# RetNet attention and a SwiGLU block on one core: the RMS norm's sum over partitions taken by VectorE block turns and one 16-column product

## The chip, the cores and the metric

The kernel runs on one NeuronCore of one Trainium2 chip. The metric is the device time of one launch in microseconds (us). Before the change three runs gave 1104.73 us as their median (1101.4 to 1110.42).

The engines are named as the profile names them: PE is TensorE (PEld its loading of weights), DVE is VectorE, ACT is ScalarE, POOL is GpSimd, SP is SyncE, which here only issues transfers. Each engine works through its own queue in the order in which the program issued to it.

## What is computed

```python
# q, k, v: (8, 8, 576, 64); tokens 4608, d_model 512, d_ff 1536, all float32
scores = scale * q @ k.T;  ret = scores * Dmat           # per head, decay matrix
attn   = ret @ v                                          # then (B,H,S,D) -> x (4608, 512)
rms = sqrt(mean(x * x, axis=-1) + 1e-6)
xn  = x / rms * rms_g
g = xn @ w_gate;  val = xn @ w_val
out = (g * sigmoid(g) * val) @ w_out
```

The part that changes is the middle one: for each token, the sum of the squares of its 512 features, the reciprocal root of that sum, and the multiplication of x by it and by `rms_g`.

## The kernel before, in words

**Layout.** The 4608 tokens are cut into nine units of 512 (`u` = 0 to 8). A unit's x lies in on-chip memory as `[128, 4, 512]`: the 512 features are four chunks of 128 partitions, the tokens run along the columns. A sum over a token's features is therefore a sum over four chunks, which adding four tiles does, and over 128 partitions, which no column-wise operation does.

**Attention.** 32 jobs (8 batches, 4 pairs of heads). A job's `slot` (L431) issues the values of the job before, its own scores and states to PE, then `weigh` (L320) and `sums` (L334) to DVE, and `carried` (L391), whose last step copies into x. For the first eight jobs (units 0 and 1) q and k are turned by PE (`turn`, L222).

**The feed-forward part.** Units 0 and 1 multiply with plain weights (`up_plain`, L694) while the same weights are rounded and prepared on the fly (`rounding`, L1191, whose steps `exponent` on ACT, `mantissa` and `join` on DVE handle 36 half blocks one after the other; after every fourth `join` of an up block, POOL adds the block's sums, L1130). Units 2 to 8 use a product scheme with seven instead of eight sub-products: `up` (L635) has six rounds of seven products, `across` (L781) has seven products of the output matrix. In `across`, POOL makes the sums of the left operands (`inner_sums`, L759) and DVE adds the results.

**The norm before, units 2 to 8.** `square` (L456, ACT) and `gather` (L464, DVE) give one `[128, 512]` tile with a row of partial sums in each partition. `root_1` (L499) multiplies it on PE by a matrix of ones, `[128,128] x [128,512]`, so that every partition holds every token's sum; then ACT and DVE compute a reciprocal root on all 512 columns by an integer guess and steps of an iteration (ACT L506, L509, L516; DVE L510, L513, L517); `root_2` (L522) has the last two DVE operations (L526, L529). `scale_x` (L537) multiplies the four chunks of x by the result (L548), which lies in on-chip SBUF, and `sums_of_x` (L553) makes the sums for the next unit's `up`.

**The norm before, units 0 and 1.** `norm_1` (L476): eight PE products of one column each (L481) turn the sums so that tokens lie on partitions; ACT adds epsilon (L486), POOL takes the power -0.5 (L487), `diagonals` (L490, ACT, L495) spreads the 4 columns over four diagonal matrices, and `scale_x` multiplies ones by them on PE (L546) so that PSUM holds the rows, which L548 reads.

**What sets the order.** There is no scheduler: queues run in the order of issue. For units 0, 1 and the first half of unit 2's preparation the order is the string `PLAN` (L1158), read word by word: `T` turn, `S` slot, `C` close, `Q` square, `G` gather, `N` norm_1, `D` diagonals, `X` scale_x, `U` up_plain (unit, block, quarter), `w` one step of the rounding, `a` one ACT step of it, `A` one product of `across`, `R` root_1, `Y` root_2, `M` sums_of_x, `k` the constant `rms_k`. For the units after that the loop at L1282 sets it: in the last round of `up` the four squares and gathers ride on the first four products, `root_1(u + 1)` on the fifth (i == NHP), and in `across` `root_2(u + 1)` comes at i == 2, the four `scale_x` at i = 3 to 6, `sums_of_x` at i == 8.

**PSUM.** Eight banks of 512 columns are handed out in turn (`bank`, L89); a bank that was freed earliest is given next.

Of the kernel before, what the change touches and what calls it, by code (L numbers as in the profile page):

```python
# [10 lines left out]
F32 = mybir.dt.float32  # L11
U32 = mybir.dt.uint32
AF = mybir.ActivationFunctionType
# [31 lines left out]
def kernel(  # L45
# [56 lines left out]

    ones = const.tile([P, P], F32, name="ones")
    ident = const.tile([P, P], F32, name="ident")
    mean_w = cell("mean_w", 1.0 / DM)
    mhalf = cell("mhalf", -0.5)
    eps = cell("eps", EPS)
    most = cell("most", 1151.0 + 7.5 / 16)
    top = cell("top", 255.0 * 2.0**23)
    guess = cell("guess", 0x5F1FFFF9 + 2.0**22 * np.log2(DM))  # L110
# [364 lines left out]

    def norm_1(u):  # L476

        ms = bank(f"ms_{u}")
        for s in range(NS):
            for i, sq in enumerate(t_of[u]):  # L480
                nc.tensor.matmul(  # L481
                    ms[:, s : s + 1], lhsT=sq[:, s * P : s * P + P], rhs=mean_w,
                    start=(i == 0), stop=(i == 1),
                )
        r = tmp.tile([P, NS], F32, tag="r", name=f"r_{u}", bufs=1)
        nc.scalar.activation(out=r, in_=ms[:, :NS], func=AF.Relu, bias=eps)  # L486
        nc.gpsimd.tensor_tensor(out=r, in0=r, in1=mhalf.to_broadcast([P, NS]), op=ALU.pow)  # L487
        t_of[u] = r

    def diagonals(u):  # L490

        r = t_of[u]
        t_of[u] = row(f"diag_{u}")
        for s in range(NS):
            nc.scalar.activation(  # L495
                out=t_of[u][:, s * P : s * P + P], in_=ident, func=AF.Copy, scale=r[:, s : s + 1]
            )

    def root_1(u):  # L499


        y = t_of[u]
        s = bank(f"ms_{u}")
        nc.tensor.matmul(s, lhsT=ones, rhs=y, start=True, stop=True)
        e = row(f"e_{u}")
        nc.scalar.activation(  # L506
            out=y.bitcast(U32), in_=s.bitcast(U32), func=AF.Relu, bias=guess, scale=-0.5
        )
        nc.scalar.activation(out=e, in_=y, func=AF.Square)  # L509
        nc.vector.scalar_tensor_tensor(  # L510
            out=e, in0=e, scalar=-1.0 / DM, in1=s, op0=ALU.mult, op1=ALU.mult
        )
        nc.vector.scalar_tensor_tensor(  # L513
            out=y, in0=e, scalar=K0, in1=y, op0=ALU.add, op1=ALU.mult
        )
        nc.scalar.activation(out=e, in_=y, func=AF.Square)  # L516
        nc.vector.scalar_tensor_tensor(  # L517
            out=e, in0=e, scalar=K1 * K1 / DM, in1=s, op0=ALU.mult, op1=ALU.mult
        )
        t_of[u] = y, e  # L520

    def root_2(u):  # L522


        y, e = t_of[u]
        nc.vector.scalar_tensor_tensor(  # L526
            out=e, in0=e, scalar=-10.0 / 3.0, in1=e, op0=ALU.add, op1=ALU.mult
        )
        nc.vector.scalar_tensor_tensor(  # L529
            out=y, in0=e, scalar=5.0, in1=y, op0=ALU.add, op1=ALU.mult  # L530
        )
        t_of[u] = y

    def norm_2(u):
        scale_x(u, range(NHP))
# [1 line left out]
    def scale_x(u, chunks):  # L537


        x = x_of[u]  # L540
        g = rms_k
        rb = t_of[u]
        if u < 2:
            g = rms_g
            rb = bank(f"rb_{u}")
            nc.tensor.matmul(rb, lhsT=ones, rhs=t_of[u], start=True, stop=True)  # L546
        for c in chunks:
            nc.vector.scalar_tensor_tensor(  # L548
                out=x[:, c], in0=x[:, c], scalar=g[:, c : c + 1], in1=rb,
                op0=ALU.mult, op1=ALU.mult,  # L550
            )

# [598 lines left out]
    def store_blocks(n):  # L1151
# [4 lines left out]

    IN_PSUM = range(4, 36)
    PLAN = """  # L1158
        T0 V0 a1 S0 a1 T1 a1 a1 V1 S1 T2 V2 F8 S2 V3 T3 w1 a1 w1 Q0 a1 a1 G0 Q1 a1 S3 T4 G1 V4
        a1 a1 w1 Q2 a1 S4 a1 V5 w1 T5 G2 V6 Q3 a1 a1 G3 a1 S5 w1 T6 V7 w1 Q4 a1 S6 N0 a1 w1 a1  # L1160
        D0 a1 a1 G4 a1 T7 a1 w1 a1 w1 a1 a1 a1 Q5 X0 G5 S7 w1 U000 w1 a1 a1 a1 Q6 a1 C7 G6 a1 Q7
        G7 U001 N1 w1 w1 w1 D1 U002 w1 a1 X1 a1 w1 a1 w1 w1 w1 w1 a1 a1 a1 w1 a1 U003 a1 w1 w1
# [11 lines left out]
        G9 b1 i4 Q10 k0 Q11 a1 b2 A0 i5 A0 a1 a1 G10 A0 j6 A0 A0 A0 a1 P12 A0 j7 b3 A0 j8 c2 A1  # L1174
        c0 F13 A1 v1 A1 c3 A1 j9 o0 G11 A1 A1 j10 A1 A1 j11 A1 i12 A1 R2 A1 Y2 A1 X2 M2 p1 a1 a1
        i13 A1 A1 A1 A1
    """
    TAILS = ((0, range(2)), (0, range(2, H)), (1, range(2)), (1, range(2, H)))
# [51 lines left out]
    def start():  # L1230

        tables = list(zip((causal, gv, gc, gq, gp), (_causal_table(), *_decay_tables(H, D))))

        def table(i, queue):
            t, values_ = tables[i]
            src = nc.inline_tensor(values_, name=t.tensor.name + "_table")
            queue.dma_start(out=t, in_=src.ap())

        make_identity(nc, ident)
        nc.scalar.activation(out=tick, in_=mhalf[:1], func=AF.Silu)  # L1240
        nc.vector.memset(ones, 1.0)
# [15 lines left out]
        tasks = {  # L1257
            "S": lambda j: slot(j, rest=j not in (0, FIRST)), "C": close, "T": turn, "V": scale_v,
            "P": prepare, "F": fetch, "Q": lambda j: squares.append(squared(*divmod(j, NHP))),
            "G": lambda j: gather(*squares.pop(0)), "N": norm_1, "D": diagonals, "X": norm_2,  # L1260
            "w": weights, "a": act, "d": lambda f: differences(f // 3, 2 * (f % 3)),
            "i": lambda n: inner_sums(*divmod(n, 7)),
            "j": lambda n: inner_sums(*divmod(n, 7), eng=nc.vector),
            "c": lambda b: combine(b, nc.gpsimd), "v": combine,
            "b": lambda n: (second_operand, last_operand)[n % 2](n // 2),
            "z": lambda n: store_blocks(len(halves) + 9),
            "r": refill, "W": weights_to, "A": lambda u: next(outs[u], None), "R": root_1,
            "Y": root_2, "M": sums_of_x, "o": store, "p": lambda _: later.pop()(),
            "k": lambda _: nc.vector.tensor_scalar(
                out=rms_k, in0=rms_g, scalar1=3.0 / 8.0 * K1, scalar2=None, op0=ALU.mult  # L1270
            ), "U": lambda n: up_plain(n // 100, n // 10 % 10, n % 10),
        }
# [7 lines left out]
    with tc.manual_schedule():  # L1280
        start()
        for u in range(2, NU):  # L1282
            j0 = NHP * (u + 1)
            more = u + 1 < B
            for n in range(2 * NG):
                for i, _ in enumerate(up(u, n)):
# [57 lines left out]
```

## Time and profile before

| | |
|---|---|
| Runs | 1104.73 us median of 3 (1101.4 to 1110.42) |
| Profiled execution | span 1104.5 us from the first to the last instruction; its own time isn't listed apart from the three runs, the median of which is 0.2 us above the span |
| Mean granted clock of TensorE | 0.995 |
| DMA | 243.60 MB, mean 221 GB/s |
| Products of the sevenfold scheme (L644) | 672 + 672 + 672 + 336 records of 256 columns, about 380 ns each as shown |
| Plain products (L704) | 384 records of 512 columns, 595 ns each as shown |

A float32 product stands in the trace as two PE records, and records overlap, so that their durations add up to more than the time they take; what a stretch of products takes is read from the distance of the starts. The row of a group gives its count, busy time and mean, then how long its engine idled just before it and what ended that.

### The profile page before, as it was taken

To read this page: it belongs to the slowest core of one execution; us is meant where nothing else is said; L and a number is where in the kernel's file an instruction comes from. 1 tells how busy PE (TensorE), PEld (TensorE's weight loads), DVE (VectorE), ACT (ScalarE), POOL (GpSimd) and SP (SyncE) were. 2 spreads that over 40 slices of the span, in tenths; PEclk is the share of its full clock that TensorE was granted. 3 is DMA by queue.
4 is the path that set the end of the run, shared out by engine and by line. 5 is a ranking of instruction groups with operands and counts; after the bars stand their busy time and mean duration, and the time that the engine had idled before them with its cause. 6 is when DMAs were issued, how large, how long until landed. Compare 5 with 4: busy or idle time off the path is not lost.

```text
span 1104.5 us, 24454 instructions
## 1 busy us (share of the span) xinstructions
PE 1091.5 (99%) x10102; PEld 915.1 (83%) x10102; DVE 751.7 (68%) x1219; ACT 339.7 (31%) x757; POOL 458.0 (41%) x421
## 2 busy tenths in 40 slices
PE   8899999999999999999999999999999999999998
PEld 7654444479988899889988998889888998898898
DVE  3778568877866794678657775668565935594457
ACT  5855564331124412342034303330233111211110
POOL 0026325538430196027802581239321942393236
PEclk9899999999999999999999999999999999999999
DMA  8847777696978866787678865887475755585461
GB/s 211 197 139 259 280 244 217 208 343 185 289 277 227 216 251 226 185 238 235 253 215 199 285 259 149 245 246 284 143 203 198 273 193 176 183 293 158 152 247 43
DMA packets 253871, 243.60 MB, mean 221 GB/s; under 512 B 193216, under 2 KB 213824, under 8 KB 247616
## 3 DMA queue, kind: packets, MB, share of 16 engines
q1 hardware_dynamic: 252320, 241.64, 69.1%
q8 instruction: 79, 1.29, 0.5%
q10 hardware_dynamic: 1440, 0.40, 0.2%
q14 instruction: 32, 0.26, 0.1%
HBM read 211.92 MB, written 30.08 MB: 219 GB/s over the span
## 4 chain that ended last, share of the span: by engine, by line
PE 96%; DVE 1%; issue 1%; ACT 0%; POOL 0%; POOLq 0%; DVEq 0%; ACTq 0%
PE up L704 15%; PE x L644 14%; PE w L644 13%; PE z L644 13%; PE y L644 7%; PE xo L814 6%; PE xp L814 4%; PE zo L814 4%; PE zp L814 3%; PE wo L814 2%; PE yo L814 2%; PE av L379 2%; PE wp L814 2%; PE av L399 2%; PE s L292 2%; PE yp L814 2%
## 5 line engine op out<-in xcount | busy, mean ns | idle before, releaser
L704 PE MATMUL up<-x,ring 128*128 128x512 f32 x384 | 167.1, 595 | 0.0
L644 PE MATMUL x<-x,ring 128*128 128x256 f32 x672 | 161.1, 383 | 0.0
L644 PE MATMUL w<-sums,ring 128*128 128x256 f32 x672 | 158.9, 379 | 0.0
L644 PE MATMUL z<-x,ring 128*128 128x256 f32 x672 | 158.8, 379 | 0.0
L766 POOL TENSOR_TENSOR vi<-h 128x384 f32<-128x384 f32 x32 | 39.5, 1234 | 275.2 <-DVE h L663 266.3
L704 PEld LDWEIGHTS up<-x,ring 128*128 128x128 f32 x384 | 72.3, 190 | 89.3 <-issue 84.8
L644 PEld LDWEIGHTS z<-x,ring 128*128 128x128 f32 x672 | 127.8, 190 | 19.8 <-issue 2.9
L644 PEld LDWEIGHTS w<-sums,ring 128*128 128x128 f32 x672 | 127.7, 190 | 17.2
L644 PEld LDWEIGHTS x<-x,ring 128*128 128x128 f32 x672 | 125.5, 190 | 17.4 <-ACT m L670 0.2
L771 POOL TENSOR_TENSOR vi<-h 128x384 f32<-128x384 f32 (+2 forms) x46 | 46.4, 1009 | 149.5 <-DVE h L663 149.5
L1010 POOL TENSOR_TENSOR vi<-vi 128x512 f32<-128x512 f32 (+1 forms) x77 | 78.1, 1027 | 37.9 <-DVE vi L841 21.5
L644 PE MATMUL y<-sums,ring 128*128 128x256 f32 x336 | 79.4, 379 | 0.0
L670 ACT COPY m<-x 128x512 f32<-128x512 f32 x42 | 24.6, 586 | 173.4 <-PE x L644 173.4
L651 DVE TENSOR_TENSOR h<-u,w 128x512 f32<-128x512 f32 x42 | 28.9, 688 | 67.8 <-PE w L644 67.8
L651 DVE TENSOR_TENSOR u<-m,y 128x512 f32<-128x512 f32 x42 | 28.8, 687 | 63.4 <-PE y L644 62.7
L644 PEld LDWEIGHTS y<-sums,ring 128*128 128x128 f32 x336 | 63.9, 190 | 8.6
L665 ACT ACTIVATE h<-h 128x512 f32<-128x512 f32 x63 | 39.7, 630 | 84.1 <-DVE h L651 84.1
L1130 POOL TENSOR_TENSOR vi<-vi 128x512 f32<-128x512 f32 (+1 forms) x24 | 40.7, 1696 | 30.8 <-DVE vi L1119 17.3
L651 DVE TENSOR_TENSOR u<-u,z 128x512 f32<-128x512 f32 x42 | 28.9, 688 | 33.7 <-PE z L644 33.6
L1130 POOL TENSOR_TENSOR ring<-ring 128x512 f32<-128x512 f32 x24 | 30.4, 1272 | 49.3 <-DMA w_up_blocks<-ring 44.1
L771 POOL TENSOR_TENSOR vi<-vi,h 128x384 f32<-128x384 f32 (+2 forms) x46 | 47.6, 1034 | 3.6
L771 POOL TENSOR_TENSOR vi<-h,vi 128x384 f32<-128x384 f32 (+2 forms) x46 | 46.9, 1019 | 3.6
(314 smaller groups left out, 2086.5 us busy)
## 6 DMA issues: line engine op xcount, KB each, us to landing
ring<-w_out_blocks SPq DMA_DIRECT2D x59, 1344.0 KB, 6.4
ring<-w_up_blocks SPq DMA_DIRECT2D x42, 1792.0 KB, 7.7
w_out_blocks<-vi SPq DMA_DIRECT2D x21, 448.0 KB, 5.9
out_dram<-vi SPq DMA_DIRECT2D x64, 128.0 KB, 3.0
qraw<-in_q_dram SPq DMA_DIRECT2D x96, 72.0 KB, 5.1
kraw<-in_k_dram SPq DMA_DIRECT2D x96, 72.0 KB, 2.5
k<-in_k_dram SPq DMA_DIRECT2D x48, 128.0 KB, 2.9
v<-in_v_dram SPq DMA_DIRECT2D x48, 128.0 KB, 2.8
```

The lines of the kernel that those rows point to most:

```text
L292: nc.tensor.matmul(s[e][side(odd), i * L : i * L + L], lhsT=d["kT"][side(e), c * L : c * L + L], rhs=d["qT"][side(e), c * L : c * L + L], ...
L379: mm = nc.tensor.matmul(av[odd][column(j, odd, e), i * L : i * L + L], lhsT=d["v"][side(odd), i, e] if c < NC - 1 else d["vt"][:, e], rhs= ...
L644: nc.tensor.matmul(ps[:, i * HU : i * HU + HU], lhsT=w[:, PLACE[blk], c, i * P : i * P + P], rhs=t_of[u][blk][:, c], start=(start and i == ...
L651: nc.vector.tensor_tensor(out=o, in0=a, in1=pairs_of(ps), op=ALU.add)
L665: nc.scalar.activation(out=o, in_=c, func=AF.Silu)
L670: nc.scalar.copy(out=s1, in_=pairs_of(x_))
L704: nc.tensor.matmul(ps, lhsT=w[:, PLACE[blk], c % 2, i * P : i * P + P], rhs=x_of[u][:, c], start=(c == 0), stop=(c == NHP - 1),)
L766: eng.tensor_tensor(out=i1, in0=x12, in1=x11, op=ALU.subtract)
L771: eng.tensor_tensor(out=o[:, c], in0=a[:, c], in1=b[:, c], op=op)
L814: nc.tensor.matmul(ps, lhsT=lhs[:, c], rhs=w[:, s, c], start=((nm, s // 4) not in first), stop=False, skip_group_check=True,)
L1010: eng.tensor_tensor(out=t[:, :, o], in0=t[:, :, x], in1=t[:, :, y], op=ALU.add)
L1130: nc.gpsimd.tensor_tensor(out=t[o], in0=t[x], in1=t[y], op=op)
```

## The change

All nine units now have the same norm:

1. `gather` adds all four chunks for every unit, epsilon included (units 0 and 1 used to leave the last addition to PE).
2. `fold` (DVE): one reduction of the `[128, 512]` tile with a turn of 32x32 blocks. The tile is read as 16 blocks of 32 columns; in each group of 32 partitions, partition j receives the sum over the group's 32 partitions of column j of the block. Result: `[128, 16]`, four partial sums per token, one in each partition group.
3. `meet` (PE): one product of 16 columns with `alike`, a matrix that has a one where two partitions agree modulo 32. Each partition j of each group then holds the whole sum of token 32 b + j in column b (PSUM).
4. `root` (DVE): the guess and the iteration, now eight operations on 16 columns, none of them on ACT; then one block turn of the `[128, 16]` result, broadcast 32 times along the columns, which writes the `[128, 512]` rows into a PSUM bank.
5. `scale_x` reads those rows from PSUM for every unit. No product follows in units 0 and 1.
6. `same_rows` makes `alike` once, from the identity. The constants `mean_w`, `eps` and `guess` go.
7. The order: `K` (same_rows) is put behind the first slot; in `PLAN` the fold of unit 0 stands before slot 5, the product before slot 6, the root behind it; for unit 1 the fold stands before the second product of unit 0 and the product and the root behind it; `k` (rms_k) moves to just before X0. In the loop, `fold` takes the place of `root_1` (i == NHP), `meet` stands at i == 6, behind the last product of `up`, and `root` takes the place of `root_2`.

```diff
     def gather(u, c, sq):
-        if c == NHP - 1 and u > 1:
+        if c == NHP - 1:
             nc.vector.scalar_tensor_tensor(
                 out=sq, in0=t_of[u], scalar=EPS * DM / P, in1=sq, op0=ALU.add, op1=ALU.add
             )
-        elif u < 2 and c == NHP - 1:
-            sq = (t_of[u], sq)
...
-    def norm_1(u):
-    def diagonals(u):
-    def root_1(u):
-    def root_2(u):
...
+    def fold(u):
+        t = column_of(f"fold_{u}")
+        nc.vector.tensor_reduce(
+            out=t, in_=t_of[u].rearrange("p (b j) -> p b j", j=SQ), axis=mybir.AxisListType.X,
+            op=ALU.add, apply_transpose=True,
+        )
+        t_of[u] = t
+    def same_rows(_):
+        t = tmp.tile([P, SQ], F32, tag="d", name="d", bufs=1)
+        nc.vector.tensor_reduce(
+            out=t, in_=ident.rearrange("p (a b) -> p b a", b=SQ), axis=mybir.AxisListType.X,
+            op=ALU.add,
+        )
+        nc.vector.tensor_copy(
+            out=alike.rearrange("p (a b) -> p a b", b=SQ),
+            in_=t.unsqueeze(1).to_broadcast([P, P // SQ, SQ]),
+        )
+    def meet(u):
+        t = t_of[u]
+        s = t_of[u] = bank(f"ms_{u}")[:, :NB]
+        nc.tensor.matmul(s, lhsT=alike, rhs=t, start=True, stop=True)
+    def root(u):
+        s = t_of[u]
+        y, e = column_of(f"y_{u}"), column_of(f"e_{u}")
+        def step(o, a, c, b, op0, op1=ALU.mult):
+            nc.vector.scalar_tensor_tensor(out=o, in0=a, scalar=c, in1=b, op0=op0, op1=op1)
+        nc.vector.tensor_scalar(
+            out=y.bitcast(U32), in0=s.bitcast(U32), scalar1=-0.5, scalar2=GUESS,
+            op0=ALU.mult, op1=ALU.add,
+        )
+        nc.vector.tensor_tensor(out=e, in0=y, in1=y, op=ALU.mult)
+        step(e, e, -1.0 / DM, s, ALU.mult)
+        step(y, e, K0, y, ALU.add)
+        nc.vector.tensor_tensor(out=e, in0=y, in1=y, op=ALU.mult)
+        step(e, e, K1 * K1 / DM, s, ALU.mult)
+        step(e, e, -10.0 / 3.0, e, ALU.add)
+        step(y, e, 5.0, y, ALU.add)
+        t_of[u] = bank(f"rows_{u}")
+        nc.vector.transpose(
+            out=t_of[u].rearrange("p (b j) -> p b j", j=SQ),
+            in_=y.unsqueeze(2).to_broadcast([P, NB, SQ]),
+        )
...
     def scale_x(u, chunks):
-        g = rms_k
         rb = t_of[u]
-        if u < 2:
-            g = rms_g
-            rb = bank(f"rb_{u}")
-            nc.tensor.matmul(rb, lhsT=ones, rhs=t_of[u], start=True, stop=True)
...
-                out=x[:, c], in0=x[:, c], scalar=g[:, c : c + 1], in1=rb,
+                out=x[:, c], in0=x[:, c], scalar=rms_k[:, c : c + 1], in1=rb,
...
     PLAN = """
-        T0 V0 a1 S0 a1 T1 ... G3 a1 S5 w1 T6 V7 w1 Q4 a1 S6 N0 a1 w1 a1
-        D0 a1 a1 G4 a1 T7 a1 w1 a1 w1 a1 a1 a1 Q5 X0 G5 S7 w1 U000 w1 a1 a1 a1 Q6 a1 C7 G6 a1 Q7
-        G7 U001 N1 w1 w1 w1 D1 U002 w1 a1 X1 ...
+        T0 V0 a1 S0 K0 a1 T1 ... G3 N0 a1 S5 w1 T6 V7 w1 Q4 a1 R0 S6 Y0 a1 w1 a1
+        a1 a1 G4 a1 T7 a1 w1 a1 w1 a1 a1 a1 Q5 k0 X0 G5 S7 w1 U000 w1 a1 a1 a1 Q6 a1 C7 G6 a1 Q7
+        G7 N1 U001 R1 w1 w1 Y1 w1 U002 w1 a1 X1 ...
...
-        j11 A1 i12 A1 R2 A1 Y2 A1 X2 M2
+        j11 N2 A1 i12 A1 R2 A1 Y2 A1 X2 M2
...
                         elif i == NHP:
-                            root_1(u + 1)
+                            fold(u + 1)
+                        elif i == 6:
+                            meet(u + 1)
...
                 if i == 2:
-                    root_2(u + 1)
+                    root(u + 1)
```

More of the change, by code (lines that the diff above doesn't have):

```diff
@@ L104 @@
     ident = const.tile([P, P], F32, name="ident")
-    mean_w = cell("mean_w", 1.0 / DM)
     mhalf = cell("mhalf", -0.5)
-    eps = cell("eps", EPS)
     most = cell("most", 1151.0 + 7.5 / 16)
     top = cell("top", 255.0 * 2.0**23)
-    guess = cell("guess", 0x5F1FFFF9 + 2.0**22 * np.log2(DM))
+    GUESS = float(0x5F1FFFF9 + 2.0**22 * np.log2(DM))
+    NB = U // SQ
+    alike = const.tile([P, P], F32, name="alike")
     causal = const.tile([P, L], F32, name="causal")
@@ L474, in gather @@
         t_of[u] = sq
-    def norm_1(u):
[L478 to L488, printed above, removed]
@@ L490, in diagonals @@
-    def diagonals(u):
[L492 to L497, printed above, removed]
-    def root_1(u):
[L502 to L507, printed above, removed]
-        )
-        nc.scalar.activation(out=e, in_=y, func=AF.Square)
-        nc.vector.scalar_tensor_tensor(
-            out=e, in0=e, scalar=-1.0 / DM, in1=s, op0=ALU.mult, op1=ALU.mult
-        )
-        nc.vector.scalar_tensor_tensor(
-            out=y, in0=e, scalar=K0, in1=y, op0=ALU.add, op1=ALU.mult
-        )
-        nc.scalar.activation(out=e, in_=y, func=AF.Square)
-        nc.vector.scalar_tensor_tensor(
-            out=e, in0=e, scalar=K1 * K1 / DM, in1=s, op0=ALU.mult, op1=ALU.mult
-        )
-        t_of[u] = y, e
@@ L522, in root_2, with column_of @@
-    def root_2(u):
-        y, e = t_of[u]
-        nc.vector.scalar_tensor_tensor(
-            out=e, in0=e, scalar=-10.0 / 3.0, in1=e, op0=ALU.add, op1=ALU.mult
-        )
[L529 to L532, printed above, removed]
+    def column_of(name):
+        return tmp.tile([P, NB], F32, tag="c", name=name, bufs=3)
+    def fold(u):
[3 more added lines that the diff above has]
+            op=ALU.add, apply_transpose=True,
+        )
+        t_of[u] = t
@@ L1158 @@
     PLAN = """
-        T0 V0 a1 S0 a1 T1 a1 a1 V1 S1 T2 V2 F8 S2 V3 T3 w1 a1 w1 Q0 a1 a1 G0 Q1 a1 S3 T4 G1 V4
-        a1 a1 w1 Q2 a1 S4 a1 V5 w1 T5 G2 V6 Q3 a1 a1 G3 a1 S5 w1 T6 V7 w1 Q4 a1 S6 N0 a1 w1 a1
-        D0 a1 a1 G4 a1 T7 a1 w1 a1 w1 a1 a1 a1 Q5 X0 G5 S7 w1 U000 w1 a1 a1 a1 Q6 a1 C7 G6 a1 Q7
-        G7 U001 N1 w1 w1 w1 D1 U002 w1 a1 X1 a1 w1 a1 w1 w1 w1 w1 a1 a1 a1 w1 a1 U003 a1 w1 w1
+        T0 V0 a1 S0 K0 a1 T1 a1 a1 V1 S1 T2 V2 F8 S2 V3 T3 w1 a1 w1 Q0 a1 a1 G0 Q1 a1 S3 T4 G1 V4
+        a1 a1 w1 Q2 a1 S4 a1 V5 w1 T5 G2 V6 Q3 a1 a1 G3 N0 a1 S5 w1 T6 V7 w1 Q4 a1 R0 S6 Y0 a1 w1 a1
+        a1 a1 G4 a1 T7 a1 w1 a1 w1 a1 a1 a1 Q5 k0 X0 G5 S7 w1 U000 w1 a1 a1 a1 Q6 a1 C7 G6 a1 Q7
+        G7 N1 U001 R1 w1 w1 Y1 w1 U002 w1 a1 X1 a1 w1 a1 w1 w1 w1 w1 a1 a1 a1 w1 a1 U003 a1 w1 w1
         a1 U100 w1 a1 w1 U110 w1 a1 a1 w1 a1 w1 U101 a1 w1 w1 w1 a1 a1 a1 a1 a1 w1 U010 a1 U102
@@ L1173 @@
         d2 a1 a1 a1 Q9 r2 A0 r99 A0 A0 j2 A0 G8 a1 a1 d3 b0 d4 C11 A0 i3 A0 d5 a1 A0 a1 F12 A0
-        G9 b1 i4 Q10 k0 Q11 a1 b2 A0 i5 A0 a1 a1 G10 A0 j6 A0 A0 A0 a1 P12 A0 j7 b3 A0 j8 c2 A1
-        c0 F13 A1 v1 A1 c3 A1 j9 o0 G11 A1 A1 j10 A1 A1 j11 A1 i12 A1 R2 A1 Y2 A1 X2 M2 p1 a1 a1
+        G9 b1 i4 Q10 Q11 a1 b2 A0 i5 A0 a1 a1 G10 A0 j6 A0 A0 A0 a1 P12 A0 j7 b3 A0 j8 c2 A1
+        c0 F13 A1 v1 A1 c3 A1 j9 o0 G11 A1 A1 j10 A1 A1 j11 N2 A1 i12 A1 R2 A1 Y2 A1 X2 M2 p1 a1 a1
         i13 A1 A1 A1 A1
@@ L1259, in start @@
             "P": prepare, "F": fetch, "Q": lambda j: squares.append(squared(*divmod(j, NHP))),
-            "G": lambda j: gather(*squares.pop(0)), "N": norm_1, "D": diagonals, "X": norm_2,
+            "G": lambda j: gather(*squares.pop(0)), "N": fold, "R": meet, "Y": root, "X": norm_2,
             "w": weights, "a": act, "d": lambda f: differences(f // 3, 2 * (f % 3)),
@@ L1266, in start @@
             "z": lambda n: store_blocks(len(halves) + 9),
-            "r": refill, "W": weights_to, "A": lambda u: next(outs[u], None), "R": root_1,
-            "Y": root_2, "M": sums_of_x, "o": store, "p": lambda _: later.pop()(),
+            "r": refill, "W": weights_to, "A": lambda u: next(outs[u], None), "M": sums_of_x, "o": store, "p": lambda _: later.pop()(),
             "k": lambda _: nc.vector.tensor_scalar(
                 out=rms_k, in0=rms_g, scalar1=3.0 / 8.0 * K1, scalar2=None, op0=ALU.mult
-            ), "U": lambda n: up_plain(n // 100, n // 10 % 10, n % 10),
+            ), "K": same_rows, "U": lambda n: up_plain(n // 100, n // 10 % 10, n % 10),
         }
```

## The prediction, made before the changed kernel was seen

> **What bounds the kernel now.** First the page: the span, the engines' shares, the chain that ended last.
>
> ```profile
> span 1104.5 us, 24454 instructions
> PE 1091.5 (99%) x10102; PEld 915.1 (83%) x10102; DVE 751.7 (68%) x1219; ACT 339.7 (31%) x757; POOL 458.0 (41%) x421
> PE 96%; DVE 1%; issue 1%; ACT 0%; POOL 0%; POOLq 0%; DVEq 0%; ACTq 0%
> ```
>
> PE is busy 99% of the span and makes 96% of the chain. So time taken from DVE, ACT or POOL is worth nothing where PE does not wait for them; PE time is worth itself wherever PE is not then made to wait. The second view is the chain between 380 and 392 us, a unit from the steady loop (columns: start, length, work).
>
> ```profile
> 386.10 1.73 PE w L644 x8
> 387.83 0.86 PE ms L504 x2
> 388.69 1.73 PE z L644 x8
> ```
>
> The product with the ones stands between two products without a gap: it costs its 0.86 us. The third view is the same chain from 38 to 76 us, with the norms of units 0 and 1.
>
> ```profile
> 45.44 1.88 PE ms L481 x16
> ...
> 51.68 2.00 PE rb L546 x2
> ...
> 57.45 3.63 PE up L704 x8
> ...
> 63.23 3.63 PE up L704 x8
> 66.86 1.68 PE ms L481 x16
> 68.54 3.54 PE up L704 x8
> 72.08 0.86 PE rb L546 x2
> ```
>
> Here the norm costs PE 1.88 + 2.00 and 1.68 + 0.86 us. But DVE is nearly full. Its timeline there runs from 31.4 to 50.9 with gaps of 0.2 and 0.4 us only, and its two long waits are waits for PE's rows:
>
> ```profile
> 53.72 2.72 DVE L548 SCALAR_TENSOR_TENSOR x<-x,rms_g,rb 128x512 f32<-128x512 f32 x4 [2.83 <-PE rb L546]
> 72.98 2.72 DVE L548 SCALAR_TENSOR_TENSOR x<-x,rms_g,rb 128x512 f32<-128x512 f32 x4 [3.65 <-PE rb L546]
> ```
>
> One stretch of this stage also ran at half the clock (the fields behind the engines are the granted clock, DMA share and GB/s):
>
> ```profile
> 45.70:49.15 3.45, 2.41 (x26) 2.16 (x26) 3.27 (x11) 1.79 (x5) 1.02 (x1) 1.00 0.81 146
> 49.15:52.56 3.41, 3.13 (x12) 1.90 (x12) 1.67 (x3) 2.83 (x9) 0.00 (x0) 0.50 0.82 162
> 52.56:55.98 3.42, 3.42 (x89) 2.37 (x90) 2.26 (x4) 2.09 (x4) 0.09 (x1) 0.50 0.73 170
> ```
>
> Last the groups by form, for prices (count, busy us, mean ns of one, idle before):
>
> ```profile
> L548 DVE SCALAR_TENSOR_TENSOR x<-x,rms_k,sq 128x512 f32<-128x512 f32 x28 | 36.2, 1353 | 0.2
> L548 DVE SCALAR_TENSOR_TENSOR x<-x,rms_g,rb 128x512 f32<-128x512 f32 x8 | 5.4, 743 | 6.5 <-PE rb L546 6.5
> L264 DVE STREAM_TRANSPOSE kT<-kraw 128x576 f32<-128x576 f32 x24 | 17.7, 736 | 0.0
> L526 DVE SCALAR_TENSOR_TENSOR e<-e 128x512 f32<-128x512 f32 x7 | 7.9, 1134 | 0.0
> L359 DVE COPY sum<-s 128x64 f32<-128x64 f32 x24 | 5.2, 215 | 0.0
> ```
>
> **Prices of the new operations.** The 16-column product: the one-column products of L481 took 16 records in 1.68 to 1.88 us, 0.11 each, two records to a product: 0.23 us. Above, half of L644's 256-column product (8 records in 1.73 us, so 0.43). I take 0.23, the nearer row, since 16 columns are nearer to 1 than to 256. A small DVE operation: 64 columns take 215 ns, 256 columns 417 (L1119), so 1.05 ns a column, and 16 columns 165 ns; L526 and L529, the second of which reads the first's result, start 0.03 us further apart than one lasts. So 0.2 us each, eight of them 1.6. The turn of the rows: L264's 736 ns for 576 columns gives 0.65, with the write to PSUM 0.7. `root` is 2.3 us where nothing disturbs it. The fold has no row: below it is a plain pass, 0.65 us by L264; above, if each of its 16 blocks cost a small operation of its own, 16 x 0.215 = 3.4. I take 0.65, because L264 turns the same kind of blocks in one pass.
>
> **POOL's disturbance.** L548 reading SBUF twice takes 1353 ns, beside a PSUM operand 743; L526 takes a median of 1209 where POOL works, 689 where it does not. So `scale_x` gets 0.6 us a chunk cheaper in units 2 to 8, and of the eight small operations the five that read no PSUM (two squares, the step with K0, the last two) can each lose 0.5 to 0.75 us beside POOL: 2.5 to 3.7. The Trainium skill (SBUF — State Buffer, "Who interferes with whom") says that a VectorE instruction with two SBUF inputs and a GpSimd one that reads SBUF lock each other out for a whole instruction. By that rule each of the five could wait a full POOL addition of 1.27 us (L1130 in the timeline), 6.4 us in all, and the forecast would be about 3 us later than the one from the rows.
>
> **Units 2 to 8, seven rounds.** PE loses 0.86 and gains 0.23: -0.63 us each, **-4.4 us**, if nothing new makes it wait (-3.0 with the upper price). The new waits, by the timeline of 382 to 425: the fold queues on DVE behind the h of product w, which ended at 389.3, so it ends at 390.0. The 16-column product, moved behind the last product of `up`, comes at 392.15 - 0.86 = 391.3: 1.3 us to spare, and behind it on PE is all of `across`. DVE no longer waits 0.74 + 0.70 us for ACT in `root_1` with products' results behind it, and its L510, L513, L517 (2.5 us) go, so the results that follow come some 3 us earlier. In `across`, `root` (2.3 to 6.0) and four `scale_x` (2.9) replace 1.21 + 1.37 + 5.58 = 8.2 us; `sums_of_x` ended at 416.2 and the next `up` began at 424.8, so 8 us cover it. POOL's last sums for the seventh product ended at 423.1 and PE used them at 424.1, 1 us of cover; they are less disturbed without the four long L548. ACT's three operations (1.95 us) had 4 us of idle before them: nothing. The added bank is freed when the fourth chunk is scaled, four products before its bank is wanted again. Unit 2 in `PLAN` goes the same way: X2 began at 301.2, `up` at 306.2.
>
> **Unit 0.** PE loses 3.9 us and gains 0.23, but x must be scaled by DVE before the first `up`. DVE's queue up to X0 ended at 50.9 and now gets: the wait of the last gather for its square (ACT ended it at 39.7, DVE was free at 39.0) 0.7, the gather 0.6, the fold 0.65, `root` 2.3, `rms_k` 0.2, together 4.5, less the 0.6 of gaps. X0 begins at 54.8 instead of 53.7, its first chunk is ready at 55.5, so `up` begins at 55.5 instead of 57.45: 1.9 us gained of 3.7, and PE now waits for DVE. On the way the fold pushes slot 5's weighing back by 2 us, to 42.0; PE wants it at 42.5. The root is behind slot 6 and before the next `mantissa`, which nobody needs soon.
>
> **Unit 1.** X0 ends at 57.5 (56.4 before), slot 7's sums at 60.5; PE's `carried` waits for them and ends at 61.6, not 63.2. Then on DVE: the copies into x and two gathers to 64.2, fold to 64.9, `mantissa` to 66.7, the fourth `join` to 67.3; the second product of unit 0 ends on PE at 65.2, the 16-column product at 65.5, and the next `up`, which needs that join, begins at 67.35 instead of 68.54. The one after begins at 70.9 instead of 72.94. But `Y1` sits between join and X1, and that join releases POOL's four additions of 1.27 us. Undisturbed it ends at 69.6, X1's first chunk is ready at 72.2, the sixth join at 77.4, before PE asks (74.5, 78.0): 2.0 us gained. Disturbed it is some 3 us later, X1's first chunk 75.9 and the sixth join 81.1, which product U110 began at 80.0 without: 1.1 us lost. I take a loss of **0.5 us**, nearer to the disturbed end, since the four additions start with `Y1`. Behind 73 us PE ran without a wait to 204, so what is gained or lost there stays. The three constants that go and `same_rows` (about 0.6 us, DVE idle 2.3 us between slots) lie beside loads and waits: nothing.
>
> **The sum.** 1104.5 - 4.4 + 0.5 = 1100.6, with 0.2 around the span 1100.8: **1101 us**. The median of the runs is that same 1104.73, but the runs themselves lie 9 us apart, so a median of a few is known to some 3 us.
>
> The Trainium skill (VectorE: DVE Perf Modes, "Rules for kernel authors") advises few DVE operations, since each pays its fixed cost, and calls `tensor_reduce` the slowest. The five 512-column operations that go in units 2 to 8 took 0.69 + 1.16 + 0.69 + 1.13 + 1.27 = 4.9 us by their means, the ten new ones take 3 to 7; PE covers that difference there, and in units 0 and 1, where nothing of the kind goes, it does not.
>
> **The rivals.**
> *DVE is never late in units 0 and 1.* Then PE keeps 3.65 + 2.3 = 6.0 us and the time is 1104.7 - 4.4 - 6.0 = 1094. For it: DVE's 2.8 and 3.7 us of waiting for rows go away. Against it: the queue before 50.9 has no room for 4.5 us.
> *Half clock and late weights.* The stretch at half clock followed one in which PE was busy 2.41 of 3.45 us. PE's new wait before `up` (about 2 us) and before the fourth join (1.9) could bring such a stretch on top of product time: 3.4 us lost per two windows, with the 3 us of a disturbed `Y1`: 1101 + 5 = 1106. The Trainium skill (TensorE: Matmul & The Clock Gate, Part 1) has the window at 3.4 us and free-running, so it would differ from run to run.
> *The other side, slower: the fold is not one pass.* At 3.4 us it ends at 392.7 and PE waits from 391.3, 1.4 us in each of seven rounds, 9.8; units 0 and 1 get 2 x 2.75 more on a DVE that is full: 1101 + 9.8 + 5.5 = 1116. It decides from a fold of 2 us on. Against it: L264.
> *The 16-column product is no cheaper than 0.43:* 1102.
>
> **How the numbers follow.** Likeliest (PE's saving in seven rounds, little in two): 0.57, 1097 to 1104. First rival 0.15, second 0.2, third 0.08. A measurement of this kernel tells about 1% (11 us) from no change. The range 1093 to 1109 leaves out the third rival and tails of the others, together 0.2. Faster by over 1% (below 1093.7) needs the first rival and luck: 0.1; slower by over 1% (above 1115.8) the third: 0.07; within 1%: 0.83.
>
> **What would show it.** Right: fold 0.65 us, small operations 0.2, the 16-column product 0.23 between starts, no PE wait at it; `up` of unit 0 starting near 55.5 behind a wait for L548 or its line in the new file; that wait for the root's chain. Wrong: PE waiting for the fold in the loop, a fold over 2 us, PE late in `across` for POOL's sums, more half clock.

## The result, and the profile after

The changed kernel takes 1111.15 us as the median of 19 runs (1109.04 to 1113.59), the kernel before in the same comparison 1106.41 us (19 runs, 1101.4 to 1110.42). The ratio is 1.005 with a 95% interval of 1.004 to 1.006: 4.4 to 6.6 us slower. The forecast was 1101, with a range of 1093 to 1109. The profiled execution of the changed kernel has a span of 1111.8 us at a mean granted clock of 0.994; that run took 1113.59 us, 2.4 above the median.

In what follows a product of `up_plain` has the name that `PLAN` gives it: U003 is unit 0, block 0, quarter 3. Lines of the new file: fold L480, `meet` L502, `root` L510 to L519, the turn of the rows L524, `scale_x` L538, `up_plain` L694, the mantissas L1084 to L1092, the joins L1109, POOL's sums L1120.

First the page of the changed kernel: span, shares, chain by engine.

```profile
span 1111.8 us, 24419 instructions
PE 1084.8 (98%) x10070; PEld 908.7 (82%) x10070; DVE 736.6 (66%) x1275; ACT 323.7 (29%) x726; POOL 442.0 (40%) x419
PE 90%; DVE 4%; SPq 3%; issue 1%; DMA 1%; POOL 0%; ACT 0%; POOLq 0%; DVEq 0%; ACTq 0%
```

Every engine has less work than before: PE 1091.5 to 1084.8, DVE 751.7 to 736.6, ACT 339.7 to 323.7, POOL 458.0 to 442.0. Yet the span is 7.3 us longer. PE's share of the chain fell from 96% to 90% and DVE has 4% of it, so the chain now runs over DVE in places. The view of PE's waits names one (engine, line; waited for; us in all, times, longest):

```profile
PE up L694 <- DVE x L538: 8.8, 2, 7.6
```

One wait of 7.6 us for `scale_x`. The timeline of PE shows which product waits (start, us, work, and in brackets the idle time before it and what ended it):

```profile
64.53 3.70 PE L694 MATMUL up<-x,ring 128*128 128x512 f32 x8
68.07 0.29 PE L502 MATMUL ms<-fold,alike 128*128 128x16 f32 x2
68.21 1.96 PE L694 MATMUL up<-x,ring 128*128 128x512 f32 x4
70.39 1.98 PE L694 MATMUL up<-x,ring 128*128 128x512 f32 x4 [0.22 <-DVE ring L1109]
79.97 20.41 PE L694 MATMUL up<-x,ring 128*128 128x512 f32 x41 [7.59 <-DVE x L538]
```

The row at 64.53 is U001, the two rows from 68.21 are U002, and the row at 79.97 begins with U003. All these belong to unit 0, whose x had been scaled at 59. The `scale_x` that ended at 79.9 is X1, the scaling of unit 1, which U003 does not read. What U003 shares with it is a PSUM bank: in the built program `rows_1` lies in bank 6, and the next to be given that bank, by the rule "freed earliest, given next", is the output of U003. Bank 6 is free when X1 has read its fourth chunk.

In the kernel before, U003 had the bank of U002, and the bank of unit 1's rows went to U100, the first product of unit 1, which needs X1 for its data. Nothing was visible of the hand-out there; PE ran on from U003 without a wait:

```profile
72.78 27.73 PE L704 MATMUL up<-x,ring 128*128 128x512 f32 x64
```

X1 itself is late, as the chain of what ended last shows (start, length, work):

```profile
64.65 0.95 DVE x L425 x4
65.60 0.70 DVE sq L471
...
67.14 0.71 DVE fold L480
67.85 0.58 DVE sums L1084
...
69.64 0.69 DVE ring L1109
70.34 0.09 DVE y L512
70.45 1.26 DVE e L516
71.74 0.18 DVE e L510
71.94 1.12 DVE y L510
73.08 0.19 DVE e L519
73.29 0.18 DVE e L510
73.50 0.93 DVE e L510
74.45 0.19 DVE y L510
74.67 0.73 DVE rows L524
75.39 0.57 DVE exp L1084
...
77.85 2.07 DVE x L538 x3
...
79.97 12.25 PE up L694 x22
```

DVE runs without a break from the copies into x at 64.65 to the end of X1. In the root, five operations take 0.2 us and three take 1.26, 1.12 and 0.93: these three meet POOL, whose three sums run from 70.42 to 74.40. They add what the join at 69.64 has just finished; the view puts their release down to the next instruction on DVE:

```profile
70.42 3.98 POOL L1120 TENSOR_TENSOR ring<-ring 128x512 f32<-128x512 f32 x3 [5.55 <-DVE y L512]
```

The wait has a second price. The stretches of the changed kernel around it (PE busy, PEld, DVE, ACT, POOL; then granted clock, DMA share, GB/s):

```profile
72.40:80.00 7.60, 0.04 (x1) 0.04 (x1) 7.39 (x14) 4.93 (x8) 1.91 (x2) 0.66 0.14 49
80.00:83.50 3.50, 3.50 (x4) 1.48 (x5) 3.43 (x6) 0.00 (x0) 0.00 (x0) 0.50 0.21 60
```

PE is idle for 7.6 us, and when it starts it has half the clock: U003 takes 6.08 us to the start of U100 where it took 3.53 before. The clock's own record is at 0.5 from 74.9 for 10.24 us.

Against the profile of before, by the starts of the same products: U001 +1.37 us, U002 -0.19, U003 +7.19, U100 +9.74, and +9.74 still at 198 us. From U001 to U110, the stretch in which unit 1's norm lies, PE took 16.58 us before and takes 24.95: **+8.37**, which is -1.56 for the cheaper product at L502, +7.38 from U002 to U003 (the wait, less the 0.86 us of the row product that stood there before) and +2.55 for the half clock.

The units 2 to 8 did what was forecast. The chain near unit 3's norm:

```profile
398.26 1.73 PE w L634 x8
399.98 0.13 PE ms L502 x2
400.11 1.43 PE xo L804 x12
```

The product stands without a gap between its neighbours and costs 0.13 us on the chain, not 0.86. The distance to the kernel before shrinks in steps of 0.63 to 0.71 us at each unit's norm (10.62 to 9.99 at 303 us, 7.87 to 7.24 at 970 us). Between these steps single executions drift by up to 2 us either way in the attention slots ("issue" waits), also where two kernels are the same; so the two profiles are 7.3 us apart and the medians 4.7.

### The profile page after: what moved, and what is told of

It reads as the page before. It is cut to its first block, busy times and chain, and to the rows that moved or that the text cites. A ratio compares the mean times of both kernels' runs of the same rounds, so it can differ in the third digit from the quotient of the medians.

```text
span 1111.8 us, 24419 instructions
## 1 busy us (share of the span) xinstructions
PE 1084.8 (98%) x10070; PEld 908.7 (82%) x10070; DVE 736.6 (66%) x1275; ACT 323.7 (29%) x726; POOL 442.0 (40%) x419
## 4 chain that ended last, share of the span: by engine, by line
PE 90%; DVE 4%; SPq 3%; issue 1%; DMA 1%; POOL 0%; ACT 0%; POOLq 0%; DVEq 0%; ACTq 0%
PE up L694 14%; PE x L634 13%; PE w L634 13%; PE z L634 13%; PE y L634 7%; PE xo L804 6%; PE xp L804 4%; PE zo L804 4%; PE zp L804 3%; PE wo L804 2%; PE yo L804 2%; SPq L181 2%; PE wp L804 2%; PE yp L804 2%; PE av L379 2%; PE s L292 1%
## 5 line engine op out<-in xcount | busy, mean ns | idle before, releaser
L694 PE MATMUL up<-x,ring 128*128 128x512 f32 x384 | 171.7, 607 | 9.0 <-DVE x L538 8.8
L694 PEld LDWEIGHTS up<-x,ring 128*128 128x128 f32 x384 | 73.6, 194 | 101.8 <-issue 86.2
L756 POOL TENSOR_TENSOR vi<-h 128x384 f32<-128x384 f32 x32 | 42.4, 1324 | 277.1 <-DVE h L653 267.5
L1120 POOL TENSOR_TENSOR vi<-vi 128x512 f32<-128x512 f32 (+1 forms) x24 | 40.7, 1697 | 35.9 <-DVE vi L1109 13.6
L1120 POOL TENSOR_TENSOR ring<-ring 128x512 f32<-128x512 f32 x24 | 30.5, 1273 | 61.2 <-DMA w_up_blocks<-ring 51.1
L423 ACT COPY x<-av 128x192 f32<-128x192 f32 (+6 forms) x136 | 37.8, 278 | 29.4 <-PE av L399 27.9
```

The source lines that it names most:

```text
L423: nc.scalar.copy(out=o, in_=part)
L694: nc.tensor.matmul(ps, lhsT=w[:, PLACE[blk], c % 2, i * P : i * P + P], rhs=x_of[u][:, c], start=(c == 0), stop=(c == NHP - 1),)
L756: eng.tensor_tensor(out=i1, in0=x12, in1=x11, op=ALU.subtract)
L1120: nc.gpsimd.tensor_tensor(out=t[o], in0=t[x], in1=t[y], op=op)
```

## The experiments

All are compared with the kernel before, run on the same chip; the us are the ratio's interval times 1106. Theory 1 is the bank. Rival A: VectorE's queue is full and late by itself. Rival B: the loop loses.

### Unit 1's rows in SBUF

```diff
     def root(u):
...
-        t_of[u] = bank(f"rows_{u}")
+        t_of[u] = row(f"rows_{u}") if u == 1 else bank(f"rows_{u}")
```

> The changed kernel with one edit: the rows of unit 1 go to an SBUF tile and not to a PSUM bank; nothing is moved in any queue. Theory 1 (the bank): in the changed kernel's trace PE waits 7.59 us before the product U003, which needs nothing of unit 1, because its PSUM bank is the one that holds unit 1's rows until X1 has read them (77.19 to 79.9); the products behind it then ran at half clock for another 2.5 us. With the rows elsewhere U003 begins near 72.5, U100 near 77.9 (X1's first chunk), against 86.05 now and 76.31 before: 8 us less than the changed kernel, and about 3 us (1 to 5) less than the kernel before. Rival A (the late VectorE chain alone: fold, root and mantissa on a full queue): the wait only moves to U100 and to the joins behind X1, the stretch at half clock stays, and 2 to 5 us over the kernel before are left. Rival B (the units 2 to 8 lose what was to be gained): 5 us over the kernel before, as now.

Measured: 1105.19 against 1105.61, ratio 0.9994 (0.9982 to 1.0006): the loss of 5 us is gone. PE's timeline of this kernel:

```profile
72.51 3.70 PE L694 MATMUL up<-x,ring 128*128 128x512 f32 x8 [0.69 <-ACT h L702]
77.53 3.67 PE L694 MATMUL up<-x,ring 128*128 128x512 f32 x8 [1.32 <-DVE x L538]
82.67 7.56 PE L694 MATMUL up<-x,ring 128*128 128x512 f32 x17 [1.47 <-DVE ring L1109]
```

U003 begins at 72.51 behind 0.7 us for its new predecessor in the bank (U002's output, read by ACT). What is left are 1.3 us at U100 for X1's data and 1.5 at U110 for the sixth join; no stretch at half clock follows. From U001 to U110 it is 18.65 us, +2.07. So rival A is real, but by itself it makes +2.07 of the +8.37. The time was expected 1 to 5 us below before and is 0.7 below with an interval that reaches 0.7 above.

### The new norm in units 2 to 8 alone

```diff
-        if c == NHP - 1:
+        if c == NHP - 1 and u > 1:
...
-            "G": lambda j: gather(*squares.pop(0)), "N": fold, "R": meet, "Y": root, "X": norm_2,
+            "G": lambda j: gather(*squares.pop(0)), "N": lambda u: (norm_1 if u < 2 else fold)(u), "D": diagonals, "X": norm_2,
```

(against the changed kernel; `PLAN` and `scale_x` for units 0 and 1 are the old ones)

> The new norm in units 2 to 8 alone; units 0 and 1 have the old norm at its old places. Theory 1 (the whole loss is in unit 1): seven rounds at -0.63 us, 4.4 us less than the kernel before (3 to 5.5). Rival A (late VectorE chain in units 0 and 1): the same. Rival B (the loop loses: the root beside POOL's sums, the fold behind a result): no time gained on the kernel before, or 1 to 5 us over it.

Measured: 1102.58, ratio 0.9971 (0.996 to 0.9982), 2.0 to 4.4 us faster. Rival B is out. This kernel has the lowest median of all that were run and is faster than both the kernel before and the changed one; its interval overlaps those of three kernels below (the root behind the fifth join, all units but unit 1, and the last).

### The new norm in units 0 and 1 alone

(against the changed kernel; the loop and its norm are the old ones)

```diff
                         elif i == NHP:
-                            fold(u + 1)
-                        elif i == 6:
-                            meet(u + 1)
+                            root_1(u + 1)
...
-                    root(u + 1)
+                    root_2(u + 1)
```

> The converse: the new norm in units 0 and 1 alone, units 2 to 8 with the old one; U003 has the bank of unit 1's rows here too. Theory 1: the loss of 9.7 us at U100 with no gain behind it, 9 to 10 us over the kernel before (7 to 11), and the same wait of about 7.5 us before U003. Rival B (the loop loses): less than the 5 us of the whole change.

Measured: 1116.1, ratio 1.0094 (1.0078 to 1.011): 8.6 to 12.2 us slower. The same wait stands in its list of PE's waits, and 10.24 us at half clock with it:

```profile
PE up L730 <- DVE x L574: 7.6, 1, 7.6
```

### U003 issued ahead of X1

```diff
-        G7 N1 U001 R1 w1 w1 Y1 w1 U002 w1 a1 X1 a1 w1 a1 w1 w1 w1 w1 a1 a1 a1 w1 a1 U003 a1 w1 w1
+        G7 N1 U001 R1 w1 w1 Y1 w1 U002 w1 a1 U003 X1 a1 w1 a1 w1 w1 w1 w1 a1 a1 a1 w1 a1 a1 w1 w1
```

> The changed kernel with U003 issued ahead of X1, so that it takes a bank that is free and X1 (rows still in PSUM) stands behind U003 in the issue; VectorE's own order is as it was. Theory 1: as with the rows in SBUF, no wait before U003, U100 near 78, some 3 us (1 to 5) less than the kernel before. Rival A: the wait moves to U100 and 2 to 5 us over the kernel before are left. A third reading, that PSUM as the place of the rows costs time by itself (bank or no bank), would have this kernel slow and the one with rows in SBUF fast.

Measured: 1108.16, ratio 1.0026 (1.0016 to 1.0036), so slower than before and not the gain that was expected. The last row of PE's timeline tells why:

```profile
67.81 5.42 PE L694 MATMUL up<-x,ring 128*128 128x512 f32 x12 [0.22 <-DVE ring L1109]
77.99 12.43 PE L694 MATMUL up<-x,ring 128*128 128x512 f32 x25 [4.76 <-DVE ring L1109]
```

U002's second half and U003 run from 67.81 to 73.2 as theory 1 has it. Then U100 waits 4.76 us, but for the fifth join (it ends at 77.94) and not for X1's first chunk, ready at 75.4; yet block 0's weights were joined long before. In the built program U100's bank is that of `exp_4`, an operand of the fifth join. It is a second case of the same thing, which the expectation did not have in it. The third reading (PSUM costs time by itself) is out: U003 ran without a wait with the rows in PSUM.

### The root ahead of the fourth join

```diff
-        G7 N1 U001 R1 w1 w1 Y1 w1 U002 w1 a1 X1
+        G7 N1 U001 R1 w1 Y1 w1 w1 U002 w1 a1 X1
```

> The changed kernel with the root of unit 1 issued ahead of the fourth join, whose end releases POOL's three additions; by this U003 also gets another bank, and U100, which needs X1 anyway, gets that of the rows. Theory 1: no wait before U003; the root takes 2.4 us as in unit 0 and not 5.1 us; the fourth join comes 3 us later and PE waits that long in the middle of U002; U100 begins 2.7 us later than in the kernel before; with 4.4 us from units 2 to 8 some 2 us less than the kernel before (0 to 4). Rival C (the small operations are slow of themselves, POOL or not): the root takes 5 us here too, and the time is about 1 us over the kernel before.

Measured: 1105.76 against 1106.16, ratio 0.9996 (0.9983 to 1.0009): 1.9 us faster to 1.0 slower, which alone decides nothing between theory 1 and rival C. PE waits 2.35 us within U002, for the fourth join, and at U003 only 0.69 us, for ACT's read of U002 and not for X1:

```profile
72.22 1.98 PE L694 MATMUL up<-x,ring 128*128 128x512 f32 x4 [2.35 <-DVE ring L1109]
74.89 15.29 PE L694 MATMUL up<-x,ring 128*128 128x512 f32 x35 [0.69 <-ACT h L702]
```

The root's three operations that were slow in the changed kernel, here:

```profile
69.41 0.18 DVE L516 TENSOR_TENSOR e<-y 128x16 f32<-128x16 f32 x1
69.82 0.17 DVE L510 SCALAR_TENSOR_TENSOR y<-e,y 128x16 f32<-128x16 f32 x1
70.44 0.17 DVE L510 SCALAR_TENSOR_TENSOR e<-e 128x16 f32<-128x16 f32 x1
```

POOL's sums begin only behind the join, at 72.24, in this kernel:

```profile
72.24 3.98 POOL L1120 TENSOR_TENSOR ring<-ring 128x512 f32<-128x512 f32 x3 [7.54 <-DVE ring L1109]
```

Root and turn take 2.4 us instead of 5.1. Rival C is out: it is POOL that makes them slow. The Trainium skill (SBUF — State Buffer, "Who interferes with whom") has it that a VectorE instruction with two SBUF inputs and a GpSimd one that reads SBUF exclude each other for a whole instruction. The changed kernel's trace agrees: three of the five such operations took 0.92 to 1.25 us, the others and all with a PSUM input 0.17. But not each of the five meets a new addition, which is why 2.7 us were lost and not the 6.4 that the rule taken for all five would give.

### The root behind the fifth join, rows in SBUF

```diff
-        G7 N1 U001 R1 w1 w1 Y1 w1 U002 w1 a1 X1 a1 w1 a1 w1
+        G7 N1 U001 R1 w1 w1 w1 U002 w1 a1 w1 Y1 X1 a1 a1 w1
```

(with the edit of the first experiment)

> The rows of unit 1 in SBUF, and its root issued behind the fifth mantissa and join with X1 directly behind it. VectorE's work is the same, but the fifth join comes ahead of the root. Theory 1 with the sum of the first runs (with rows in SBUF alone U100 was 1.3 us late and U110 another 1.7 us for the sixth join): X1 begins at about 75.5, its first chunk and U100 at 76.2, the sixth join ends near 81; of the 3 us at most 1.3 are left, and the time is 3 to 4 us less than the kernel before (2 to 5), 2 us less than with the rows in SBUF alone. Rival A (a full VectorE queue, whatever its order): the same time as with rows in SBUF alone, equal to the kernel before within 1 us.

Measured: 1104.08 against 1106.16, ratio 0.9982 (0.9969 to 0.9996), 0.4 to 3.4 us faster than before. From U001 to U110 16.95 us, against 18.65 with the rows in SBUF alone: the order of the same work was worth 1.7 us in the trace. Left are 0.7 us at U003 for ACT's read of U002 and a wait of 0.9 us for the sixth join:

```profile
79.31 11.00 PE L694 MATMUL up<-x,ring 128*128 128x512 f32 x25 [0.94 <-DVE ring L1109]
```

Against rival A's strong form (whatever the order) the trace speaks plainly; the times of the two kernels, measured in two comparisons, are not far enough apart for that.

### All units but unit 1

```diff
-        if c == NHP - 1:
+        if c == NHP - 1 and u != 1:
...
-            "G": lambda j: gather(*squares.pop(0)), "N": fold, "R": meet, "Y": root, "X": norm_2,
+            "G": lambda j: gather(*squares.pop(0)), "N": lambda u: (norm_1 if u == 1 else fold)(u), "D": diagonals, "X": norm_2,
```

(against the changed kernel; `PLAN` and `scale_x` for unit 1 are the old ones)

> The new norm in all units but unit 1, which has the old one at its old place. Theory 1: unit 0 gains 0 to 2 us, units 2 to 8 gain 4.4: 5 us less than the kernel before (3.5 to 6.5), and 0 to 2 less than with units 2 to 8 alone, which measured 3.2 less. Rival A (unit 0 loses as well, since PE waits there for X0): more than with units 2 to 8 alone, 0 to 3 us less than the kernel before.

Measured: 1104.31, ratio 0.9986 (0.9974 to 0.9997), 0.3 to 2.9 us faster. That is less than units 2 to 8 alone gave, so unit 0 did not gain but lost, if anything; the two intervals overlap. From U001 to U110 it is 16.58, exactly that of before.

### The same conflict given to the kernel before

```diff
+    def pad(_):
+        nc.tensor.matmul(
+            bank("pad")[:, :1], lhsT=ones, rhs=ones[:, :1], start=True, stop=True
+        )
...
-        G7 U001 N1 w1 w1 w1 D1 U002 w1 a1 X1 a1 w1 a1 w1 w1 w1 w1 a1 a1 a1 w1 a1 U003 a1 w1 w1
+        G7 U001 N1 w1 w1 w1 D1 U002 w1 a1 X1 a1 w1 a1 w1 w1 w1 w1 a1 a1 a1 w1 a1 B0 U003 a1 w1 w1
...
-            ), "U": lambda n: up_plain(n // 100, n // 10 % 10, n % 10),
+            ), "B": pad, "U": lambda n: up_plain(n // 100, n // 10 % 10, n % 10),
```

(against the kernel before)

> The converse on the kernel before: nothing of the change, but one PE product of one column into a bank of its own is issued ahead of U003, so that the hand-out moves on by one and U003 gets the bank of unit 1's rows, while U100 gets one that is free by then. Theory 1: U003 waits for the end of X1 (75.6) and begins 2.9 us later than its 72.78; what PE does behind it stays that late: 3 us over the kernel before (2 to 5, the upper part if a stretch at half clock comes with it). Any theory in which the bank plays no part: the 0.1 us of the added product.

Measured: 1109.99 against 1106.16, ratio 1.0034 (1.0019 to 1.0048), 2.1 to 5.3 us slower. One product of one column, in a kernel without any of the change:

```profile
69.45 1.02 PE L551 MATMUL rb<-diag,ones 128*128 128x512 f32 x2
70.31 0.38 PE L223 MATMUL pad<-ones 128*128 128x1 f32 x2
73.29 17.00 PE L709 MATMUL up<-x,ring 128*128 128x512 f32 x39 [2.60 <-DVE x L553]
```

U003 waits 2.60 us for X1, and from U001 to U110 PE takes 19.57 instead of 16.58: +2.99, as expected. So the bank alone, with nothing else of the change, makes this wait. The profiled run took 1107.07 us at a granted clock of 0.998, the median of the twelve is 1109.99. Of the eight runs above 1109 us seven have a granted clock of 0.992 to 0.996, so a stretch at half clock may have followed the wait there; no trace shows it.

### Unit 0 alone

```diff
-        if c == NHP - 1 and u > 1:
+        if c == NHP - 1 and u != 1:
...
-            "G": lambda j: gather(*squares.pop(0)), "N": norm_1, "D": diagonals, "X": norm_2,
+            "G": lambda j: gather(*squares.pop(0)), "N": lambda u: (norm_1 if u == 1 else fold)(u), "D": diagonals, "X": norm_2,
```

(against the kernel before; `PLAN` and `scale_x` for unit 0 are those of the change)

> The new norm in unit 0 alone; units 1 to 8 have the old one. The prediction on record had 1.9 us gained there. The traces so far, measured from slot 4's weighing to the start of U001, give 28.7 us in the mean of seven profiles with the new norm in unit 0 (27.5 to 29.6) against 28.2 in three with the old one (26.5 to 29.6): nothing gained, because PE's waits ahead of U000 are followed by a stretch at half clock inside U000 in most of them. Theory 1: the kernel before within 1.5 us, rather above it (0 to 2). The step on record: 1.9 us less.

Measured: 1107.52 against 1106.16, ratio 1.002 (1.0008 to 1.0033), 0.9 to 3.6 us slower. In its profile U001 began 27.8 us after slot 4's weighing; the eight profiles with the new norm in unit 0 now have a mean of 28.6, the four with the old one 28.7. The times say that unit 0 loses about 2 us, the profiles show neither gain nor loss beyond their spread of 4 us.

### Unit 0 old, unit 1 in the better order, units 2 to 8 new

```diff
-        if c == NHP - 1:
+        if c == NHP - 1 and u > 0:
...
-        G7 N1 U001 R1 w1 w1 Y1 w1 U002 w1 a1 X1 a1 w1 a1 w1
+        G7 N1 U001 R1 w1 w1 w1 U002 w1 a1 w1 Y1 k0 X1 a1 a1 w1
```

(against the changed kernel, with the edit of the first experiment; unit 0 as before)

> The old norm in unit 0, the new one in unit 1 (rows in SBUF, root and X1 behind the fifth join) and in units 2 to 8. By the traces so far unit 1 so ordered costs 0.4 us from U001 to U110, units 2 to 8 gain 4.4 by their products and measured 3.2 by themselves: 3 to 4 us less than the kernel before (2 to 5), that is no better than units 2 to 8 alone. If the half clock in unit 0 were a matter of chance and not of its norm, this kernel would do no better than the one with the same order in unit 1 and the new norm in unit 0, 2 us less than the kernel before.

Measured: 1104.64 against 1106.16, ratio 0.9989 (0.9976 to 1.0002): 2.7 us faster to 0.2 slower, less than the 3 to 4 expected and not better than units 2 to 8 alone. From U001 to U110 it is 16.97. Even in the best order that I found, unit 1's new norm takes PE no less time than the old one, though PE has 2.4 us less to do there: what PE no longer does, it mostly waits: 1.1 us for the fourth and sixth joins and 0.7 for ACT's read of U002.

## Why the prediction was wrong

**The step that failed** is this sentence: "The added bank is freed when the fourth chunk is scaled, four products before its bank is wanted again." In units 2 to 8 no product waited for `scale_x`. I took the sentence from the loop and did not follow the bank of `rows_1` through `PLAN`, where the next to be given that bank is U003, which needs nothing of unit 1 and had to wait for X1's end. The loss of 0.5 us taken for unit 1 let U003 follow U002 at once, at 70.9; it began at 79.97. From U001 to U110 unit 1 measured +8.4 us: 7.4 from U002 to U003, nearly all of it the wait, and 2.6 for the half clock behind it, less 1.6 for the cheaper product. With the bank out of the way +2.07 are left, and the conflict alone, put into the kernel before, costs 2.99. The two do not add up to 8.4: the later X1 (it ended at 79.9, in the kernel before at 75.7) makes the bank's wait longer, and in the traces only the long wait has half clock behind it.

**The rest of unit 1** was as forecast. The loss of 0.5 us was counted at U110 and had 1.6 us gained at U001 in it (61.6 instead of 63.2), so from U001 to U110 it stands for +2.1; with the bank out of the way 2.07 are measured. The mechanism was the one forecast (`Y1` between join and X1, disturbed by POOL), and the disturbance was sized right, 2.7 us against 2.5 to 3.7, though POOL had three additions left to make there and not four. The fourth join ended at 70.3 and not at 67.3, and X1's first chunk came at 77.9 where the forecast's disturbed case had 75.9, because U001 began at 64.5 and not at 61.6: this execution was 1.1 us late by slot 4 already, and U000 ran at half clock, 5.40 us and not 3.63.

**Unit 0 is the second miss.** "X0 begins at 54.8" was right against its queue: 20.2 us after slot 4's weighing were worked out, 20.6 are in the trace. The gain of 1.9 at U000, of which the forecast kept 1.6 at U001, did not come: U000 began 1.4 us earlier than before on that scale and then ran at half clock, so that U001 began 0.3 us later. The rows for the window before it (54.36 to 57.77, with PE busy for 1.43 us of 3.41) and for the next show how:

```profile
54.36:57.77 3.41, 1.43 (x18) 0.80 (x15) 3.31 (x8) 2.90 (x5) 0.00 (x0) 1.00 0.75 162
57.77:61.19 3.42, 3.42 (x5) 1.51 (x5) 3.35 (x8) 0.00 (x0) 0.00 (x0) 0.51 0.85 243
```

This was the second rival, to which I had given 0.2: the half clock came at the first of its two places, and in unit 1 behind the bank's wait instead of behind the late join. Its 1106 was too low, since it had no bank in it. By the times unit 0 lost 2 us, and the cause is not settled. Half clock near U000 is no mark of the new norm: of the eight profiles with it in unit 0 seven have a stretch of 3.41 us, five of them inside U000; of the four with the old norm three have 6.83 us, ahead of U000 and not inside it.

**Units 2 to 8:** right by the records, in sum and in its parts: -0.63 us a unit. By the times it is 2.0 to 4.4 us, so the 4.4 of the forecast lies at the end of the interval. `meet` costs 0.13 on the chain (0.23 forecast), the fold 701 ns (0.65), a small operation 0.17 (0.2), the rows 727 ns (0.7), and `scale_x` fell from 1353 to 743 ns as worked out:

```profile
L538 DVE SCALAR_TENSOR_TENSOR x<-x,rms_k,rows 128x512 f32<-128x512 f32 x36 | 24.5, 743 | 0.3
L524 DVE STREAM_TRANSPOSE rows<-y 128x512 f32<-128x512 f32 x9 | 6.5, 727 | 0.3
L480 DVE TRANSPOSE_TENSOR_REDUCE fold<-sq 128x16 f32<-128x512 f32 x9 | 6.3, 701 | 0.1
```

The third rival (a fold in several passes) is out with that last row.

**"Behind 73 us PE ran without a wait to 204, so what is gained or lost there stays"** was right too: the 9.74 us stood unchanged to 198 us.

The sum as it should have been, by the traces: -4.4 for units 2 to 8, +8.4 for unit 1, 0 to 2 for unit 0, in all +4 to +6; measured 4.4 to 6.6. The two parts timed by themselves are less consistent: -3.2 for units 2 to 8 and +10.4 for units 0 and 1 make 7.2, with an uncertainty of some 2 us. The sum also began too low: no run shows its 0.2 us around the span. Every run of the record whose span is listed took 1.7 to 1.9 us more than its span, and the kernel before has a median of 1106.4 in 19 runs, not 1104.7.

## What to carry to other kernels

A buffer that is added to a pool with a fixed order of hand-out changes the owner of every buffer behind it. Wherever the order of work is not a loop, list who gets the added buffer next and when its last reader is done; a product can then wait for data that it never reads, and in the profile this shows as a wait for an instruction that is not among its operands. And what is followed through for the steady loop has to be followed once more for the start, where the queues are full: here, by the traces, seven rounds gained 4 us and one unit lost 8.

## What the hardware did that I had not expected

An idle PE costs more than the idle time if it is long. In the traces the waits of 2.35 and 2.60 us (root ahead of the fourth join; the conflict in the kernel before) were followed by full clock, the one of 4.76 us (U003 ahead of X1) by 3.41 us at half clock, the two of 7.6 us by 10.24 us, which is three times the 3.41 us of the shortest stretches; the products behind these two took 2.4 to 2.6 us longer. The Trainium skill (TensorE: Matmul & The Clock Gate, Part 1) gives a free-running window of 3.4 us, after an idle one of which the clock is halved, and this agrees with the lengths of 3.41, 6.83 and 10.24 us. But the stretch ahead of U000 was not idle: 1.43 us of PE work in 3.41 were followed by half clock as well, so here it did not take an idle window. No run here took the half clock away and left the wait of 7.6 us, so its share is read from the records and not shown by an experiment.

Small operations cost little: 0.17 us for 16 columns, eight of them and a turn of `[128, 512]` in 2.4 us. And a sum over 32 partitions with the turn of 32x32 blocks is one pass, 701 ns for 512 columns.
